# An expert layer's first product on 512-row tiles by seven quarter products instead of eight

## The chip, the cores and the metric

The kernel runs on one core of a Trainium2 chip. A core has five engines with a queue each: TensorE (PE in the profile; its weight loads are shown as PEld), VectorE (DVE), ScalarE (ACT), GpSimd (POOL) and SyncE (SP, which here only starts DMA transfers). Each works its queue in order, and they wait for each other by semaphores. Matmul results go to PSUM, of which this kernel uses eight banks of 128 x 512 float32, seven of them in one rotating pool.

The metric is the time of one execution in microseconds on the device. Three runs of the kernel before gave 1623.6 us as the median (1623.3 to 1626.15).

## The reference

Two blocks follow each other. The first is a filter along the sequence by a real Fourier transform (8 sequences of 2496 rows, 256 columns); the second a mixture of 8 experts with one expert for each row. All data is float32.

```python
X = np.fft.rfft(x, axis=1)
F = (filt_r + 1j * filt_i)[None, :, :]
y = np.fft.irfft(X * F, n=x.shape[1], axis=1)

x = y.reshape(B * S, D)                          # 19968 rows, D = 256
logits = x @ w_gate                              # 8 experts
expert_idx = np.argmax(logits, axis=1)
gate_w = softmax(logits)[arange(N), expert_idx]  # with 1e-9 in the denominator
for e in range(E):                               # the rows of expert e
    h = np.maximum(x_e @ w1[e], 0.0)             # 256 -> 1024
    y_e = h @ w2[e]                              # 1024 -> 256
out = gate_w[:, None] * y                        # in the rows' old order
```

## The kernel before

**Transform.** It is done as matmuls in four stages, A to D (`stage_a` to `stage_d`), for one of the eight sequences after the other; between the stages, data goes to DRAM and back in another layout (tensors `zd` and `ud`). Stage B multiplies its products by the filter with four VectorE operations (L366 to L370), and stage C reads the result. For the first sequence GpSimd does the fourth of them, and the layouts are changed by transposes in SBUF.

**Routing.** `turn_y`, `logits` and `route` take stage D's rows, choose the expert by many small VectorE operations and write each row, with its index and gate, into a DRAM table sorted by expert (`rows`), by indirect DMAs that GpSimd starts (L607, 128 rows or fewer each).

**Experts.** When the rows of one more sequence are in the table, `tile_map` finds which tiles of rows of one expert can be worked. A tile has 512, 256 or 128 rows. `GROUPS` sets their numbers ahead: 28 tiles of 512 rows, 14 of 256 and 23 of 128, the last two kinds mostly at the end. For each tile:

- `rows_in` loads the rows (`xg`), `weights` loads w1 and w2 of the expert in two halves each (`w1t`, `w2t`, 512 KB a half), all on SP's queue;
- `turn_x` transposes the rows (L737) into `xT`, which has the 256 columns of x as two blocks of 128 partitions, `dh`;
- `hidden(i, k)` makes 128 of the 1024 hidden columns for the whole tile: two matmuls, one for each `dh`, added up in a bank (L744), then a relu into `hT` on VectorE or ScalarE (L747, L748);
- `result(i, j)` makes 128 rows of output by eight matmuls with `hT` as weights and `w2t` as the moving side (L758), scales them with the gate (L762, L763) and writes them to their places with an indirect DMA of GpSimd (L764).

`turn_x` of the next tile stands between the last `hidden` and the first `result` of a tile where the rows have been loaded by then.

**Order of the work.** The order on TensorE, VectorE, ScalarE and SP is the order in which the program emits it. A loop at the end emits a step of the transform or one of the experts, by a simple clock of its own (`now`), costs written beside each step, and a credit: each transform step gives the experts `share()` times its cost. `either` picks VectorE or ScalarE for an evacuation by which would be free first in that clock. `side` emits pieces of routing between. `prefetch` emits the loads when a buffer count allows. GpSimd's order is left to the framework. When the transform is over, its memory is given to w1 buffers for the 128-row tiles (`late["w1"]`) and to all of w2.

Of the kernel before, what the change touches and what calls it, by code (L numbers as in the profile page):

```python
# [22 lines left out]
E = 8  # L23
# [111 lines left out]
def kernel(  # L135
# [215 lines left out]
    def stage_b(b, f):  # L351
# [11 lines left out]
        yw = sb.tile([P, 2, D], F32, tag="yw", name="yw")  # L363
# [261 lines left out]
    def tile_map(b, rows, n, last):  # L625
# [21 lines left out]
        tau = pools["moe"].tile([1, n], F32, tag=f"tau{n}", name="tau", bufs=1)  # L647
        past = pools["moe"].tile([1, n, E - 1], F32, tag=f"past{n}", name="past", bufs=1)
# [5 lines left out]
        ef = pools["moe"].tile([1, n], F32, tag=f"ef{n}", name="ef", bufs=1)  # L654
# [5 lines left out]
        rf = pools["moe"].tile([1, n], F32, tag=f"rf{n}", name="rf", bufs=1)  # L660
# [24 lines left out]
    work, idt, gts, xgs, xts, w1t, w2t, hs = [], {}, {}, {}, {}, {}, {}, {}  # L685
# [21 lines left out]

    def weights(h, second):
# [10 lines left out]
        if second:  # L719
            w2t[h] = pools["moe"].tile([P, FH2, D], F32, tag="w2t", name="w2t", bufs=3)  # L720
            nc.sync.dma_start(out=w2t[h], in_=moe_w2[bass.ds(ev, 1), k].rearrange("o p i d -> p (o i) d"))
        else:
            pool, bufs = (late["w1"], 8) if i >= SHORT else (pools["moe"], 3)
            w1t[h] = pool.tile([P, DH, F // 2], F32, tag="w1t", name="w1t", bufs=bufs)
            nc.sync.dma_start(out=w1t[h], in_=moe_w1[bass.ds(ev, 1), k].rearrange("o p i f -> p (o i) f"))

    def turn_x(i):
# [6 lines left out]
        for dh in range(DH):  # L734
# [3 lines left out]
            evac(xts[i][:, dh, :n * P].rearrange("p (j q) -> p j q", j=n), pt[:, :n], n * P)  # L738

    def hidden(i, k):  # L740
        m = work[i][0] * P
        p = bank()
        for dh in range(DH):
            mm(p[:, :m], lhsT=w1t[2 * i + k // FH2][:, dh, k % FH2 * P:(k % FH2 + 1) * P], rhs=xts[i][:, dh, :m],  # L744
               start=(dh == 0), stop=(dh == DH - 1))
        hT = pools["moe"].tile([P, 512], F32, tag="hT", name="hT", bufs=9)
        either(m, lambda: nc.vector.tensor_scalar_max(hT[:, :m], p[:, :m], 0.0),  # L747
               lambda: nc.scalar.activation(hT[:, :m], p[:, :m], AF.Relu))  # L748
        hs.setdefault(i, []).append(hT)

    def result(i, j):
# [4 lines left out]
        for k in range(FT):  # L756
            w2 = late["w2s"][:, bass.ds(ev, 1), k, :] if i >= SHORT else w2t[2 * i + k // FH2][:, k % FH2, :]
            mm(p[:, :D], lhsT=hs[i][k][:, j * P:(j + 1) * P], rhs=w2, start=(k == 0), stop=(k == FT - 1))  # L758
        ys = pools["moe"].tile([P, D], F32, tag="ys", name="ys", bufs=4)
# [126 lines left out]
    def experts():  # L886

        for i in range(NT):
# [18 lines left out]
    def share():  # L907

        known = sum(7.1 * t[0] for t in work[used["w2"] // 2:])
# [71 lines left out]
```

## Time and profile before

| | |
|---|---|
| median of three runs | 1623.6 us |
| profiled execution | 1628.1 us, of which its span is 1626.4 us |
| TensorE busy | 1570.7 us, 97% of the span |
| VectorE, ScalarE, GpSimd busy | 423.1, 518.5, 358.2 us |
| mean granted TensorE clock | 0.987 |
| first product of the experts, records of 512, 256 and 128 columns (L744) | 896, 448, 736 |
| second product of the experts (L758) | 2240 + 368 records |
| read from and written to HBM | 208.44 MB, 80.90 MB |

The profile is of one execution. A float32 matmul appears in it as two weight loads (LDWEIGHTS) and two MATMUL records. A line of a group gives the line of the kernel, engine, operation, what is written and read, the shape, the count, then busy us in all and mean ns of one, then the engine's idle time just before, with what ended it. Matmuls overlap in the pipeline, so a record's length is more than its share of the time; the pace is read from the starts. A line of the timeline gives start and length in us; "x32" is 32 instructions merged. A line of a table of stretches gives the bounds, the length, the busy time of PE, PEld, DVE, ACT and POOL with the number of instructions, then the granted TensorE clock, the DMA engines' busy share and GB/s.

### The profile page before, as it was taken

The page shows a single profiled execution, that of the slowest core. Times are in us where ns is not written, and L with a number is a line of the kernel's source. Part 1 is how long each engine was busy: PE and PEld are TensorE (multiplying, and loading weights), DVE is VectorE, ACT ScalarE, POOL GpSimd, SP SyncE. Part 2 cuts the span into 40 slices and gives each one's busy share as a digit, 9 for nine tenths or more (in the row PEclk, how much of TensorE's full clock was granted, in tenths as well). Part 3 has the DMA queues.
Part 4 walks back from the last instruction along what each step waited for, and adds up shares of the span by engine and source line. Part 5 has one row for each costly group of instructions (what it writes and reads, how often), then busy time and mean ns, then how long its engine had stood idle before and what let it go on. Part 6 is the DMA issues. An engine that isn't in the chain of part 4 may idle for free.

```text
span 1626.4 us, 21714 instructions
## 1 busy us (share of the span) xinstructions
PE 1570.7 (97%) x7094; PEld 1143.6 (70%) x7094; DVE 423.1 (26%) x1418; ACT 518.5 (32%) x1149; POOL 358.2 (22%) x373
## 2 busy tenths in 40 slices
PE   8988899999999999999999899999999999999998
PEld 6645667787566666666666566667666678889997
DVE  4676571624412422235222111300000000000000
ACT  4434343333322232322233232122222222333433
POOL 1131312404213321023213205411111011111111
PEclk9999999999999999999999999999999999999999
DMA  9679796887935584357434624433344347565551
GB/s 283 185 198 293 234 329 196 244 262 241 289 121 163 167 250 138 114 152 191 144 106 129 178 89 142 145 112 112 133 151 153 129 142 229 187 214 184 172 182 46
DMA packets 119700, 289.89 MB, mean 178 GB/s; under 512 B 17387, under 2 KB 58484, under 8 KB 119469
## 3 DMA queue, kind: packets, MB, share of 16 engines
q1 hardware_dynamic: 100373, 245.18, 49.9%
q0 software_dynamic: 19216, 43.33, 7.7%
q8 instruction: 58, 0.95, 0.2%
q14 instruction: 53, 0.43, 0.1%
HBM read 208.44 MB, written 80.90 MB: 178 GB/s over the span
## 4 chain that ended last, share of the span: by engine, by line
PE 90%; DMA 4%; DVE 3%; issue 2%; SPq 0%; ACT 0%; POOL 0%; POOLq 0%; ACTq 0%; DVEq 0%
PE bank L758 34%; PE bank L744 34%; PE bank L405 4%; PE bank L359 3%; PE bank L344 3%; PE bank L384 3%; PE bank L737 2%; PE bank L477 2%; DMA fin<-zd 1%; PE lt L491 1%; DMA fin<-ud 1%; DMA ud<-uo 1%; PE bank L424 1%; DVE yw L368 1%; DVE yw L367 1%
## 5 line engine op out<-in xcount | busy, mean ns | idle before, releaser
L744 PE MATMUL bank<-xT,w1t 128*128 128x512 f32 (+2 forms) x2080 | 592.0, 436 | 0.0
L758 PE MATMUL bank<-w2t,hT 128*128 128x256 f32 x2240 | 503.9, 382 | 2.6 <-issue 2.6
L744 PEld LDWEIGHTS bank<-xT,w1t 128*128 128x128 f32 x2080 | 338.9, 191 | 206.2 <-issue 183.7
L758 PEld LDWEIGHTS bank<-w2t,hT 128*128 128x128 f32 x2240 | 423.9, 191 | 70.2 <-issue 14.2
L764 POOL DMA_INDIRECT out_dram<-ys,idt x163 | 160.6, 985 | 917.2 <-ACT ys L763 624.4
L748 ACT ACTIVATE hT<-bank 128x512 f32<-128x512 f32 (+2 forms) x520 | 227.3, 438 | 369.3 <-PE bank L744 333.4
L607 POOL DMA_INDIRECT rows<-yo,row x176 | 175.5, 997 | 303.5 <-DVE row L587 73.6
L763 ACT ACTIVATE ys<-bank,gts 128x256 f32<-128x256 f32 x157 | 74.3, 474 | 500.0 <-PE bank L758 447.9
L241 DVE COPY xT<-bank 128x128 f32<-128x128 f32 (+2 forms) x53 | 25.1, 473 | 586.1 <-PE bank L737 459.6
L366 DVE TENSOR_TENSOR ys<-bank,ht 128x512 f32<-128x512 f32 x80 | 55.1, 689 | 131.0 <-PE bank L359 88.2
L405 PE MATMUL bank<-fin,tds 120*117 120x256 f32 (+1 forms) x308 | 77.6, 391 | 12.0 <-DMA fin<-ud 12.0
L758 PE MATMUL bank<-w2s,hT 128*128 x368 | 83.2, 379 | 0.0
L405 PEld LDWEIGHTS bank<-fin,tds 120*117 120x117 f32 (+1 forms) x308 | 55.6, 185 | 37.0 <-issue 20.4
L384 PE MATMUL bank<-ys,tcs 128*128 128x512 f32 x126 | 67.0, 614 | 10.8 <-DVE ys L370 6.1
L344 PE MATMUL bank<-fin,tas 117*120 117x512 f32 x154 | 74.5, 603 | 0.0
L758 PEld LDWEIGHTS bank<-w2s,hT 128*128 128x128 f32 x368 | 68.1, 190 | 8.3
L359 PE MATMUL bank<-fin,tbs 128*128 128x256 f32 x280 | 73.2, 385 | 0.8 <-DMA fin<-zd 0.8
L359 PEld LDWEIGHTS bank<-fin,tbs 128*128 128x128 f32 x280 | 52.3, 192 | 21.5 <-issue 15.5
L241 ACT COPY uo<-bank 128x512 f32<-128x512 f32 x70 | 41.1, 587 | 62.7 <-PE bank L384 36.7
L367 DVE SCALAR_TENSOR_TENSOR yw<-bank,ht 64x512 f32<-64x512 f32 x80 | 55.4, 693 | 1.1
L368 DVE TENSOR_TENSOR yw<-bank,ht 64x512 f32<-64x512 f32 x80 | 54.7, 684 | 1.1
L241 ACT COPY yo<-bank 117x512 f32<-117x512 f32 x70 | 40.6, 589 | 40.7 <-PE bank L405 38.5
(126 smaller groups left out, 877.6 us busy)
## 6 DMA issues: line engine op xcount, KB each, us to landing
w1t<-in_moe_w_dram SPq DMA_DIRECT2D x130, 512.0 KB
w2t<-in_moe_w_dram SPq DMA_DIRECT2D x84, 512.0 KB
fin<-in_x_dram SPq DMA_DIRECT2D x40, 512.0 KB
fin<-zd SPq DMA_DIRECT2D x70, 256.0 KB
ud<-uo SPq DMA_DIRECT2D x70, 256.0 KB
zd<-zo SPq DMA_DIRECT2D x35, 480.0 KB
fin<-ud SPq DMA_DIRECT2D x35, 480.0 KB
xg<-rows SPq DMA_DIRECT2D x28, 544.0 KB
```

The costliest lines, as they stand in the source:

```text
L241: either(n, lambda: nc.vector.tensor_copy(o, i), lambda: nc.scalar.copy(out=o, in_=i))
L344: mm(p[:TK, :], lhsT=tas, rhs=xt[:TP, j:j + 2, :], start=True, stop=True)
L359: mm(p[:, i * D:(i + 1) * D], lhsT=tbs[:, f + i, :], rhs=zi[:, j + i, :], start=True, stop=True)
L367: nc.vector.scalar_tensor_tensor(out=yw[:HP], in0=z2[HP:], scalar=-1.0, in1=fi, op0=ALU.mult, op1=ALU.mult)
L384: mm(p, lhsT=tcs[:, 1, :], rhs=ys, start=True, stop=True)
L405: mm(p[:TP, i * D:(i + 1) * D], lhsT=tds[:k, i0 + j + i, :], rhs=ui[:k, j + i, :], start=True, stop=True)
L607: sc = nc.gpsimd.indirect_dma_start(out=rowsd, out_offset=bass.IndirectOffsetOnAxis(ap=at, axis=0), in_=what, in_offset=None,)
L744: mm(p[:, :m], lhsT=w1t[2 * i + k // FH2][:, dh, k % FH2 * P:(k % FH2 + 1) * P], rhs=xts[i][:, dh, :m], start=(dh == 0), stop=(dh == DH - 1))
L748: lambda: nc.scalar.activation(hT[:, :m], p[:, :m], AF.Relu))
L758: mm(p[:, :D], lhsT=hs[i][k][:, j * P:(j + 1) * P], rhs=w2, start=(k == 0), stop=(k == FT - 1))
L763: lambda: nc.scalar.activation(ys, p[:, :D], AF.Copy, scale=gate))
L764: nc.gpsimd.indirect_dma_start(out=out, out_offset=bass.IndirectOffsetOnAxis(ap=idt[i].bitcast(U32)[:, j, :], axis=0), in_=ys, in_offset=None,
```

## The change

On tiles of 512 rows, `hidden` gives way to `hidden_by_quarters`. It works the hidden columns in two halves (`g`; with the new layout of w1 in DRAM, a half holds columns of both halves of F, `fh`). In each half, w1 is a matrix of 2 x 2 quarters (`dh` by `fh`, 128 x 256 each), and so is the transposed tile (`dh` by half of the rows, 128 x 256 each). Their product is made of seven quarter products in place of eight, in Winograd's form of Strassen's scheme. One quarter product is two matmuls of 256 columns into one bank.

The scheme needs four sums of quarters of x for each tile (at the end of `turn_x`) and four sums of quarters of w1 for each half (`w1_sums`), all on GpSimd. The seven products are put together by seven additions on VectorE, with a bank as one operand and SBUF as the other; the first product is copied to `part` by ScalarE, and the relu becomes two operations of ScalarE on 1024 elements a partition, in place in `hT`. `w1_sums` of the next half is emitted in the middle of a half where its weights have come by the program's clock, otherwise just ahead of its own half.

For the memory, `w2t` goes from 3 to 2 buffers, `xg` from 2 to 1 (4 in the late pool for the 128-row tiles), `ys` of `result` from 4 to 3, `yw` to one buffer after the first sequence, and the small tiles of `tile_map` are shared between sizes. `hT` becomes one tile for each half, in two buffers, and `result` takes its pieces in the same order of hidden columns as before. `share` reckons 26.8 for a 512-row tile in place of 28.4.

```diff
--- before.py
+++ after.py
@@ -360,7 +360,7 @@
         z2 = p.rearrange("p (i d) -> p i d", i=2)
         ys = outs["y", b, f] = sb.tile([P, 2, D], F32, tag="ys", name="ys", bufs=3)
-        yw = sb.tile([P, 2, D], F32, tag="yw", name="yw")
+        yw = (pro if b == 0 else sb).tile([P, 2, D], F32, tag="yw", name="yw", bufs=2 if b == 0 else 1)
...
+        most = max(m for group in GROUPS for _, m in group)
+        tau = pools["moe"].tile([1, most], F32, tag="tau", name="tau", bufs=1)[:, :n]
...
-        xg = xgs[i] = pools["moe"].tile([P, 4, DR], F32, tag="xg", name="xg")
+        xg = xgs[i] = (late["w1"] if i >= SHORT else pools["moe"]).tile([P, 4, DR], F32, tag="xg", name="xg", bufs=4 if i >= SHORT else 1)
...
         if second:
-            w2t[h] = pools["moe"].tile([P, FH2, D], F32, tag="w2t", name="w2t", bufs=3)
+            w2t[h] = pools["moe"].tile([P, FH2, D], F32, tag="w2t", name="w2t", bufs=2)
...
             pool, bufs = (late["w1"], 8) if i >= SHORT else (pools["moe"], 3)
-            w1t[h] = pool.tile([P, DH, F // 2], F32, tag="w1t", name="w1t", bufs=bufs)
-            nc.sync.dma_start(out=w1t[h], in_=moe_w1[bass.ds(ev, 1), k].rearrange("o p i f -> p (o i) f"))
+            w1t[h] = pool.tile([P, DH, 2, 2 * P], F32, tag="w1t", name="w1t", bufs=bufs)
+            nc.sync.dma_start(out=w1t[h], in_=moe_w1[bass.ds(ev, 1), k].rearrange("o p i h f -> p (o i) h f"))
...
             evac(xts[i][:, dh, :n * P].rearrange("p (j q) -> p j q", j=n), pt[:, :n], n * P)
-
-    def hidden(i, k):
+        if n == 4:
+
+            b = xts[i].rearrange("p h (r c) -> p h r c", r=2)
+            t = sums[i] = pools["moe"].tile([P, 4, 2 * P], F32, tag="sums", name="sums", bufs=1)
+            nc.gpsimd.tensor_tensor(t[:, 0], b[:, 0, 1], b[:, 0, 0], op=ALU.subtract)
+            nc.gpsimd.tensor_tensor(t[:, 1], b[:, 1, 1], t[:, 0], op=ALU.subtract)
+            nc.gpsimd.tensor_tensor(t[:, 2], b[:, 1, 1], b[:, 0, 1], op=ALU.subtract)
+            nc.gpsimd.tensor_tensor(t[:, 3], b[:, 1, 0], t[:, 1], op=ALU.subtract)
+            free["p"] = max(free["p"], now[0]) + 3.0
+
+    def w1_sums(h):
+
+        w = w1t[h]
+        t = wsum[h] = pools["moe"].tile([P, 4, 2 * P], F32, tag="wsum", name="wsum", bufs=2)
+        nc.gpsimd.tensor_tensor(t[:, 0], w[:, 0, 1], w[:, 1, 1], op=ALU.add)
+        nc.gpsimd.tensor_tensor(t[:, 1], t[:, 0], w[:, 0, 0], op=ALU.subtract)
+        nc.gpsimd.tensor_tensor(t[:, 2], w[:, 0, 0], w[:, 0, 1], op=ALU.subtract)
+        nc.gpsimd.tensor_tensor(t[:, 3], w[:, 1, 0], t[:, 1], op=ALU.subtract)
+        free["p"] = max(free["p"], now[0]) + 3.0
+
+    def hidden_by_quarters(h):
...
+        i = h // 2
+        w, ws, t = w1t[h], wsum[h], sums[i]
+        b = xts[i].rearrange("p h (r c) -> p h r c", r=2)
+        hT = pools["moe"].tile([P, 2, 2, 2, 2 * P], F32, tag="hT", name="hT", bufs=2)
+        hs.setdefault(i, []).append(hT)
+        part = pools["moe"].tile([P, 2, 2 * P], F32, tag="part", name="part", bufs=1)
+
+        def product(left, right):
+            q = bank().rearrange("p (v c) -> p v c", v=2)
+            for v in range(2):
+                mm(q[:, v], lhsT=left[:, v * P:(v + 1) * P], rhs=right, start=True, stop=True)
+            return q
+
+        def add(o, q, a):
+            nc.vector.tensor_tensor(o, q, a, op=ALU.add)
+            free["v"] = max(free["v"], now[0]) + 0.7
+
+        def relu(o, q):
+            nc.scalar.activation(o, q, AF.Relu)
+            free["s"] = max(free["s"], now[0]) + 0.6
+
+        low = hT[:, 1, :, 0]
+        q = product(w[:, 0, 0], b[:, 0, 0])
+        nc.scalar.copy(out=part, in_=q)
+        free["s"] = max(free["s"], now[0]) + 0.6
+        q = product(w[:, 1, 0], b[:, 1, 0])
+        add(hT[:, 0, :, 0], q, part)
+        yield 1.71
+        q = product(ws[:, 1], t[:, 1])
+        add(part, q, part)
+        q = product(ws[:, 2], t[:, 2])
+        add(low, q, part)
+        yield 1.71
+        q = product(ws[:, 0], t[:, 0])
+        add(hT[:, 1, :, 1], q, low)
+        add(part, q, part)
+        q = product(w[:, 1, 1], t[:, 3])
+        add(low, q, low)
+        relu(hT[:, 1], hT[:, 1])
+        yield 1.71
+        q = product(ws[:, 3], b[:, 1, 1])
+        add(hT[:, 0, :, 1], q, part)
+        relu(hT[:, 0], hT[:, 0])
+        yield 0.85
+
+    def hidden(i, g, a):
+
         m = work[i][0] * P
         p = bank()
+        fh, v = divmod(a, 2)
         for dh in range(DH):
-            mm(p[:, :m], lhsT=w1t[2 * i + k // FH2][:, dh, k % FH2 * P:(k % FH2 + 1) * P], rhs=xts[i][:, dh, :m],
+            mm(p[:, :m], lhsT=w1t[2 * i + g][:, dh, fh, v * P:(v + 1) * P], rhs=xts[i][:, dh, :m],
                start=(dh == 0), stop=(dh == DH - 1))
-        hT = pools["moe"].tile([P, 512], F32, tag="hT", name="hT", bufs=9)
-        either(m, lambda: nc.vector.tensor_scalar_max(hT[:, :m], p[:, :m], 0.0),
-               lambda: nc.scalar.activation(hT[:, :m], p[:, :m], AF.Relu))
-        hs.setdefault(i, []).append(hT)
+        if a == 0:
+            hs.setdefault(i, []).append(pools["moe"].tile([P, 2, 2, 2, 2 * P], F32, tag="hT", name="hT", bufs=2))
+        hT = hs[i][g][:, fh, v].rearrange("p r c -> p (r c)")[:, :m]
+        either(m, lambda: nc.vector.tensor_scalar_max(hT, p[:, :m], 0.0),
+               lambda: nc.scalar.activation(hT, p[:, :m], AF.Relu))
...
         for k in range(FT):
             w2 = late["w2s"][:, bass.ds(ev, 1), k, :] if i >= SHORT else w2t[2 * i + k // FH2][:, k % FH2, :]
-            mm(p[:, :D], lhsT=hs[i][k][:, j * P:(j + 1) * P], rhs=w2, start=(k == 0), stop=(k == FT - 1))
-        ys = pools["moe"].tile([P, D], F32, tag="ys", name="ys", bufs=4)
+            mm(p[:, :D], lhsT=hs[i][k % 4 // 2][:, k // 4, k % 2, j // 2, j % 2 * P:(j % 2 + 1) * P], rhs=w2, start=(k == 0), stop=(k == FT - 1))
+        ys = pools["moe"].tile([P, D], F32, tag="ys", name="ys", bufs=3)
...
         i = got["x"]
-        if i < len(work) and rows_at[work[i][3]] <= now[0] and i - used["x"] < 2:
+        if i < len(work) and rows_at[work[i][3]] <= now[0] and i - used["x"] < (1 if i < SHORT else 3):
...
             if h < 2 * len(work) and rows_at[work[h // 2][3]] <= now[0] and (
-                    h - used[what] < (3 if h < 2 * SHORT else 8)):
+                    h - used[what] < ((3 if what == "w1" else 2) if h < 2 * SHORT else 8)):
                 weights(h, what == "w2")
...
-            for k in range(FT):
-                yield lambda: hidden(i, k), 0.43 * n, ("w1", 2 * i + k // FH2)
-                if (k + 1) % FH2 == 0:
-                    w1t.pop(used["w1"])
-                    used["w1"] += 1
-            xts.pop(i)
+            for g in range(2):
+                h = 2 * i + g
+                if n == 4:
+                    if h not in wsum:
+                        yield lambda: w1_sums(h), 0.0, ("w1", h)
+                    steps = hidden_by_quarters(h)
+                    for m in range(4):
+                        yield lambda: next(steps), (1.71, 1.71, 1.71, 0.85)[m], ("w1", h)
+                        if m == 1 and when.get(("w1", h + 1), now[0] + 1.0) <= now[0] and TILES[(h + 1) // 2][0] == 4:
+                            w1_sums(h + 1)
+                    wsum.pop(h)
+                else:
+                    for a in range(4):
+                        yield lambda: hidden(i, g, a), 0.43 * n, ("w1", h)
+                w1t.pop(h)
+                used["w1"] += 1
+            xts.pop(i), sums.pop(i, None)
...
     def share():
-        known = sum(7.1 * t[0] for t in work[used["w2"] // 2:])
+        known = sum(26.8 if t[0] == 4 else 7.1 * t[0] for t in work[used["w2"] // 2:])
         return min(4.0, max(0.3, (known - RESERVE) / max(left_t[0], 1.0)))
...
-        moe_w1=inputs["moe_w1"].reshape(E, DH, P, 2, F // 2).transpose(0, 3, 2, 1, 4),
+        moe_w1=inputs["moe_w1"].reshape(E, DH, P, 2, 2, F // 4).transpose(0, 4, 2, 1, 3, 5),
```

More of the change, by code (lines that the diff above doesn't have):

```diff
@@ L646, in tile_map @@
         yield
-        tau = pools["moe"].tile([1, n], F32, tag=f"tau{n}", name="tau", bufs=1)
-        past = pools["moe"].tile([1, n, E - 1], F32, tag=f"past{n}", name="past", bufs=1)
+        most = max(m for group in GROUPS for _, m in group)
+        tau = pools["moe"].tile([1, most], F32, tag="tau", name="tau", bufs=1)[:, :n]
+        past = pools["moe"].tile([1, most, E - 1], F32, tag="past", name="past", bufs=1)[:, :n]
         she = (1, n, E - 1)
@@ L653, in tile_map @@
         yield
-        ef = pools["moe"].tile([1, n], F32, tag=f"ef{n}", name="ef", bufs=1)
+        ef = pools["moe"].tile([1, most], F32, tag="ef", name="ef", bufs=1)[:, :n]
         erow = pools["moe"].tile([1, n], I32, tag=f"erow{n}", name="erow", bufs=2)
@@ L659, in tile_map @@
         yield
-        rf = pools["moe"].tile([1, n], F32, tag=f"rf{n}", name="rf", bufs=1)
+        rf = pools["moe"].tile([1, most], F32, tag="rf", name="rf", bufs=1)[:, :n]
         rrow = pools["moe"].tile([1, n], I32, tag=f"rrow{n}", name="rrow", bufs=2)
@@ L682, in tile_map @@
         work.extend((rows // P, erow[0:1, i:i + 1], rrow[0:1, i:i + 1], b) for i in range(n))
-    work, idt, gts, xgs, xts, w1t, w2t, hs = [], {}, {}, {}, {}, {}, {}, {}
+    work, idt, gts, xgs, xts, w1t, w2t, hs, sums, wsum = [], {}, {}, {}, {}, {}, {}, {}, {}, {}
     FH2 = FT // 2
```

## The prediction

> **What bounds the kernel now.** I read the page first: the busy shares, then the slices.
>
> ```profile
> PE 1570.7 (97%) x7094; PEld 1143.6 (70%) x7094; DVE 423.1 (26%) x1418; ACT 518.5 (32%) x1149; POOL 358.2 (22%) x373
> PE   8988899999999999999999899999999999999998
> DVE  4676571624412422235222111300000000000000
> ```
>
> TensorE is busy 97% of the span, and VectorE does almost nothing after about two thirds of it: the transform is over and only expert tiles are left. The chain that ended last says the same.
>
> ```profile
> PE 90%; DMA 4%; DVE 3%; issue 2%; SPq 0%; ACT 0%; POOL 0%; POOLq 0%; ACTq 0%; DVEq 0%
> ```
>
> So matmul time taken away is worth its full length, unless a wait replaces it. Next, the groups with shapes kept apart, for the prices.
>
> ```profile
> L758 PE MATMUL bank<-w2t,hT 128*128 128x256 f32 x2240 | 503.9, 382 | 2.6 <-issue 2.6
> L744 PE MATMUL bank<-xT,w1t 128*128 128x512 f32 x896 | 401.3, 596 | 0.0
> L748 ACT ACTIVATE hT<-bank 128x512 f32<-128x512 f32 x224 | 133.8, 597 | 281.3 <-PE bank L744 253.2 <-issue 23.6 <-PE bank L359 4.5
> L366 DVE TENSOR_TENSOR ys<-bank,ht 128x512 f32<-128x512 f32 x80 | 55.1, 689 | 131.0 <-PE bank L359 88.2 <-issue 13.3 <-PE bank L744 9.4
> L370 POOL TENSOR_TENSOR ys<-ys,yw 128x512 f32<-128x512 f32 x10 | 12.7, 1268 | 40.0 <-DVE yw L368 26.8 <-PE bank L344 7.9 <-PE bank L359 5.2
> L435 ACT COPY ht<-ht 64x1024 f32<-64x1024 f32 x5 | 5.2, 1045 | 0.1
> ```
>
> A matmul is two records here (896 records for 28 tiles of 8 x 2 products). Their mean overlaps the next one, so the true pace comes from the timeline of TensorE in a stretch with expert tiles alone:
>
> ```profile
> 1084.49 13.90 PE L744 MATMUL bank<-xT,w1t 128*128 128x512 f32 x32
> 1098.23 1.04 PE L737 MATMUL bank<-ident,xg 128*128 128x128 f32 x8
> 1099.10 13.98 PE L758 MATMUL bank<-w2t,hT 128*128 128x256 f32 x64
> 1112.92 13.90 PE L744 MATMUL bank<-xT,w1t 128*128 128x512 f32 x32
> ```
>
> From start to start: first product 13.74 us (0.429 a record), transposes 0.87, second product 13.82 (0.216 a record of 256 columns); one tile 28.43 us, without a gap.
>
> [...]
>
> ```profile
> 752.16:755.57 3.41, 1.64 (x11) 1.42 (x10) 3.33 (x6) 0.10 (x1) 0.84 (x1) 1.00 0.44 135
> 755.57:758.98 3.41, 3.41 (x10) 2.70 (x9) 3.20 (x16) 0.49 (x1) 0.00 (x0) 0.50 1.13 250
> ```
>
> 1.77 us without matmuls in one window (1.64 busy of 3.41), and the next runs at clock 0.50. The same after 1.87 us at 410.82, but not after 1.54 us at 107.04. So a stall over some 1.7 us inside one window costs another 1.7 us. [...]
>
> ```profile
> 31.12 1.04 ACT L435 COPY ht<-ht 64x1024 f32<-64x1024 f32 x1
> 32.19 0.58 ACT L241 COPY zi<-bank 128x512 f32<-128x512 f32 x1
> ```
>
> 1.07 us from one start to the next.
>
> **The change, part by part.** Matmuls: 32 records of 512 columns (13.74) become 56 of 256 (7 products x 2 x 2, twice) at 0.216, 12.10 us. Weight loads of 191 ns still fit under 0.216, as in the second product. Saved: 1.64 us a tile, 28 tiles, 46 us.
>
> Evacuation: eight relus on ScalarE (8 x 0.597) become, per half of F, one copy (0.59) and two relus of 1024 elements from SBUF (1.07 each), and seven adds of 0.69 on VectorE. VectorE gets 9.7 us a tile, less than the 12.1 us of matmuls beside it, so it is no bound on average. But the order is strict. I follow one unmixed tile from the start of its first half. Products end every 0.864 us, the seventh at 6.05. A VectorE op starts 0.26 us after its matmul (transposes end at 1099.10, the copy starts 1099.36) and adds follow at 0.70 (0.72 when dependent). Product 5 ends at 4.32 and has two adds (4.58, 5.28), product 6 one (5.98), product 7 one (6.68 to 7.37). ScalarE: relu of the low part 6.71, of the high part 7.78 to 8.85. Only then the copy of the second half's first product, which was ready at 7.2: 8.85 to 9.43. That copy opens the second half's adds, which now run without a pause: 9.47, 10.17, 10.89, 11.61, 12.31, 13.01, 13.71 to 14.40. Relu low 13.74 to 14.78, relu high 14.81 to 15.86. TensorE ends its products at 12.10, does the transposes (12.97) and two matmuls of the second product (13.83); the third reads the tile that the last relu writes. It starts at 15.9: a stall of 2.1 us a tile. Bounds: 1.0 if the second half carried no backlog (the first half's relu ends 2.8 after its products; 1.73 is covered)[...]. Behind that matmul stands all of TensorE's queue. The seven banks are no limit: the last add is 2.3 us behind, under three products.
>
> Clock: a 2.1 us stall puts 1.7 us into one window at (3.41 - 2.1 + 2 x 0.4) / 3.41 = 0.62 of its positions, x 1.7 us = 1.05 us a tile; none below 1.7.
>
> Unmixed tiles. In the order as built, 12 of the 28 have no transform work among them: 12 x (-1.64 + 2.1 + 1.05) = +18 us.
>
> Mixed tiles. In the other 16, transform matmuls stand between the halves, or between last product and result, and shorten the wait; a stage B in a half puts 2.8 us of VectorE work in front of the adds and lengthens it. Walking each in the built order as above I get waits of 0 to 3 us, mean 0.8, so 13 us, plus 2 for the clock, against 26 saved: -11 us.
>
> GpSimd: [...] Weight sums are needed at the third product of a half and are issued a half earlier; those of x have the 13.8 us of the second product. Hidden when unmixed: behind the last scatter they end about 5 us into the tile, needed at 7.8. In front of them in POOL's queue can stand six to eight routing scatters (1.29 us each from start to start, 8 to 10 us), in about five tiles: 0 to 15 us, I take 3.
>
> VectorE's backlog also delays stage C, which waits for stage B's products there, and relus hold ScalarE's queue while they wait for adds: bounds 0 to 15, I take 5. It is 28% busy between 440 and 1010 us and would be about 50%.
>
> At nothing: the weights' DMA has the same size and pieces of the same length. Two w2 buffers in place of three: both halves load during the next first product (12 us for some 6 us of transfer; before, the second already waited for the result's end); uncovered, a few us a tile. One xg buffer: loaded a whole tile (26 us) ahead. ys 4 to 3, hT in two tiles, yw, map tiles: their readers finish before the next writer comes. The new constant in the share shifts which step comes next; bounded by the 23 us that TensorE waits for DMA now, either way a few us, taken as 0.
>
> Sum: 18 - 11 + 3 + 5 = +15 us. The profiled execution's span of 1626.4 us becomes 1641; it took 1628.1 as a whole, 4.5 above the median of 1623.6, to which I add the same: 1638 us.
>
> **Rivals.** (1) Faster: the relu arrives less late. One mechanism, at the third matmul of each first result: if the second half carries no backlog, unmixed stalls are 1.0 us and the clock stays up. 12 x (-0.64) - 11 - 2 + 5 = -16, about 1608; with more cover in mixed tiles 1600. It decides from a mean stall under 46/28 = 1.64 us. For it: ScalarE is 32% and VectorE 26% busy. Against: the copy stands behind two relus in the built order. (2) The stall comes, the clock doesn't fall: 15 - 14 = +1, about 1625. For it: a 2.35 us stall at 130 left the clock up; it lay across two windows. (3) VectorE or GpSimd becomes the bound while the transform runs: both upper ends, +22 more, about 1660. For it: stages with VectorE at 0.5 to 0.7 already. That quarter products don't run faster is ruled out by the 0.216.
>
> **Chances.** 0.2% (3 us) is about what a measurement of this kernel tells from no change. Main case 0.48 (1630 to 1652), rival 1 0.27, rival 2 0.15 (half of it within 0.2%, the rest to either side), rival 3 0.10. Faster 0.32, same 0.09, slower 0.59. The range, 1603 to 1662, leaves out the far ends of rivals 1 and 3.
>
> **What would show it.** Right: a gap of about 2 us before the first L832 matmuls in the unmixed tiles, released by ScalarE's relu, period 28.6 us or, with a fallen clock, 30.3; first product 12.1 us; VectorE's adds without a pause in the second half. Wrong: no gap there; or gaps before the third product, released by POOL; or before stage C, by VectorE.

## The result, and the profile after

The changed kernel takes 1675.6 us (median of 4 runs, 1674.3 to 1680.4) for 1624.9 us of the kernel before beside it (1623.3 to 1627.1): 1.032 times as long, 95% interval 1.029 to 1.034. The forecast of 1638 us had the sign right and the size wrong: +51 us, not +15, and outside the range. The profiled execution spans 1672.5 us; before, 1626.4. All that follows accounts for these 46.1 us.

The page of the changed kernel, its busy shares and four of its slices:

```profile
PE 1549.9 (93%) x7766; PEld 1278.4 (76%) x7766; DVE 691.8 (41%) x1789; ACT 535.6 (32%) x1114; POOL 597.9 (36%) x709
PE   8988979999899989998999998888999999999998
DVE  5585662634734474456655443344333330000000
POOL 2131433306434443345436546643444421111111
PEclk9998989999999999999999999998999999999999
```

TensorE works 20.8 us less and is idle 66.9 us more (122.6 us of the span, before 55.7). The granted clock was 0.976, before 0.987: at 1 minus the clock, times the span, that is 40.1 us, before 21.1. So three terms make the sum: 66.9 us of idle time, 19.0 us of lowered clock, and 39.8 us of matmul time saved, which is what remains (busy time less the clock's part: 1509.8 for 1549.6). 66.9 + 19.0 - 39.8 = 46.1.

The groups of instructions that are new, with what ended the idle time before them:

```profile
L832 PE MATMUL bank<-w2t,hT 128*128 128x256 f32 x2240 | 518.6, 388 | 45.2 <-ACT hT L784 42.3
L780 DVE TENSOR_TENSOR hT<-bank,part 128x512 f32<-128x512 f32 x168 | 115.4, 687 | 322.3 <-ACT part L789 161.2
L784 ACT ACTIVATE hT<-hT 128x1024 f32<-128x1024 f32 x112 | 113.8, 1051 | 297.7 <-DVE hT L780 273.1
L776 PE MATMUL bank<-sums,wsum 128*128 128x256 f32 x672 | 161.3, 386 | 9.5 <-POOL wsum L755 8.1
```

The second product (L832), which waited for no other engine before, waits 42.3 us for the relu that closes a half. The relu waits for the adds, the adds for the copy: a loop over three engines that the kernel before did not have. A wait of 8.1 us for GpSimd's sums stands apart from it.

Where it lies. I cut both traces at the same tiles, counted from 0, where their transposes start (the second product of the tile before comes just after them): tile 1, the first of 512 rows; tiles 2 to 22, five of 256 rows and sixteen of 512 among the transform's work; tiles 23 to 26; tiles 27 to 33, the last of 512 rows. Columns: the stretch, its length, then busy time of TensorE, its weight loads, VectorE, ScalarE and GpSimd, the clock and the DMA. First before, then after:

```profile
239.21:256.07 16.86, 16.86 (x42) 8.15 (x42) 4.78 (x24) 5.35 (x9) 7.90 (x8) 0.87 0.85 285
256.07:1007.79 751.72, 739.73 (x3138) 511.29 (x3136) 232.97 (x773) 233.03 (x472) 188.56 (x190) 0.99 0.58 173
1007.79:1126.65 118.86, 116.30 (x421) 77.82 (x420) 17.69 (x104) 28.74 (x53) 31.90 (x33) 0.99 0.39 127
1126.65:1325.61 198.96, 198.96 (x730) 133.48 (x729) 5.88 (x21) 50.02 (x91) 27.36 (x28) 1.00 0.41 139
```

```profile
237.42:264.04 26.62, 18.56 (x66) 14.89 (x66) 13.59 (x36) 4.52 (x7) 16.30 (x20) 0.74 0.69 212
264.04:1027.65 763.61, 724.14 (x3521) 585.70 (x3520) 382.72 (x975) 243.87 (x458) 326.18 (x382) 0.98 0.57 168
1027.65:1171.15 143.50, 120.37 (x517) 100.73 (x516) 58.38 (x162) 31.46 (x48) 69.28 (x85) 0.92 0.34 106
1171.15:1369.69 198.54, 189.30 (x897) 164.81 (x896) 73.00 (x120) 52.06 (x77) 84.07 (x108) 1.00 0.41 138
```

Tile 1 costs 9.8 us more, tiles 2 to 22 cost 11.9, tiles 23 to 26 cost 24.6, tiles 27 to 33 gain 0.4; before tile 1 it is -1.8, after tile 33 +2.0. (Which piece of the transform falls between which tiles differs a little, so the second and third figures are good to a few us.) Half of the loss is in four tiles in which TensorE has almost no transform work left. Most of the idle time there is the wait for the relu, once in each second product, 16.4 us of 23.1:

```profile
1033.39 14.70 PE L832 MATMUL bank<-w2t,hT 128*128 128x256 f32 x60 [3.69 <-ACT hT L784]
1067.94 16.18 PE L832 MATMUL bank<-w2t,hT 128*128 128x256 f32 x60 [5.58 <-ACT hT L784]
1103.39 14.90 PE L832 MATMUL bank<-w2t,hT 128*128 128x256 f32 x60 [3.69 <-ACT hT L784]
1143.06 16.17 PE L832 MATMUL bank<-w2t,hT 128*128 128x256 f32 x60 [3.41 <-ACT hT L784]
```

In tiles 2 to 22 this wait is 14.9 us. The other waits that are new there are for VectorE: 18.4 us in all (stage C 7.8, routing 5.0, transposes behind an add 4.2 and smaller ones) for 2.8 before, while those for DMA fell from 9.2 to 1.5.

At tile 1 TensorE waits for the sums of w1. GpSimd's queue, then TensorE's:

```profile
243.57 1.01 POOL L607 DMA_INDIRECT rows<-yo,row  x1 [3.88 <-DVE cnt L588]
244.61 0.73 POOL L754 TENSOR_TENSOR wsum<-w1t 128x256 f32<-128x256 f32 x1
...
247.33 0.71 POOL L755 TENSOR_TENSOR wsum<-wsum,w1t 128x256 f32<-128x256 f32 x1
```

```profile
248.10 4.45 PE L776 MATMUL bank<-sums,wsum 128*128 128x256 f32 x12 [6.13 <-POOL wsum L755]
```

The sums stood behind one routing scatter that itself waited 3.88 us for VectorE; those of the second half then stood behind five more scatters, and TensorE waited another 1.93 us.

One clean tile, on TensorE's timeline:

```profile
1171.15 1.04 PE L738 MATMUL bank<-ident,xg 128*128 128x128 f32 x8
1172.03 1.03 PE L832 MATMUL bank<-w2t,hT 128*128 128x256 f32 x4
1174.38 13.22 PE L832 MATMUL bank<-w2t,hT 128*128 128x256 f32 x60 [1.32 <-ACT hT L784]
1187.43 1.89 PE L776 MATMUL bank<-xT,w1t 128*128 128x256 f32 x8
```

The first product ran from 1159.07 to 1171.15, 12.08 us for 13.74 before: the seven products save what they should. The second product takes 15.40 us from start to start for 13.82: a gap of 1.32 us before its third matmul, and 0.26 us more. 1.66 saved, 1.58 given back. Every one of these seven tiles shows the same 1.32.

The four tiles (23 to 26) show why a loop over in-order queues is worse than its clean walk. GpSimd's timeline (the first and the last of routing's 14 scatters, then the first scatter of a result), then ScalarE's:

```profile
1063.81 1.01 POOL L607 DMA_INDIRECT rows<-yo,row  x1 [0.19 <-issue]
...
1083.06 0.97 POOL L607 DMA_INDIRECT rows<-fill,pad  x1 [0.31 <-issue]
1084.34 0.99 POOL L838 DMA_INDIRECT out_dram<-ys,idt  x1 [0.30 <-issue]
```

```profile
1080.77 0.47 ACT L837 ACTIVATE ys<-bank,gts 128x256 f32<-128x256 f32 x1 [2.99 <-PE bank L832]
1089.22 0.47 ACT L837 ACTIVATE ys<-bank,gts 128x256 f32<-128x256 f32 x1 [7.98 <-DMA out_dram<-ys,idt]
1089.60 0.58 ACT L789 COPY part<-bank 128x512 f32<-128x512 f32 x1
```

The results of a tile were ready from 1073.5 us on, but their scatters stood behind 20 us of routing's scatters. The fourth result found none of the three `ys` buffers free, ScalarE's queue stood 7.98 us, and behind it stood the copy that opens the next tile's adds. One tile later it is VectorE:

```profile
1120.13 0.69 DVE L780 TENSOR_TENSOR hT<-bank,part 128x512 f32<-128x512 f32 x1 [10.34 <-ACT part L789]
...
1124.29 0.14 DVE L630 TENSOR_TENSOR av<-cnt,done 1x8 f32<-1x8 f32 x1
1124.46 0.70 DVE L631 TENSOR_SCALAR av_i<-av 1x8 int32<-1x8 f32 x1
1125.20 0.65 DVE L632 TENSOR_SCALAR av_i<-av_i 1x8 int32<-1x8 int32 x1
...
1127.85 0.67 DVE L780 TENSOR_TENSOR hT<-bank,hT 128x512 f32<-128x512 f32 x1
```

Between the third and the fourth add of a half, 1124.29 to 1127.85, stands routing's list of tiles, ten small instructions; others stand before the second and after the sixth. The seven adds of that half took from 1120.13 to 1132.91, not 5. Four of the ten were slow: L631, L632, L636 and L641 took 0.65 to 0.70 us beside GpSimd's sums of 1124.42 to 1127.3, and 0.14 to 0.19 in the list before, from 1108.25 on. The adds, with one input from PSUM, took 0.68 to 0.69 us in the clean tiles, beside the sums and without them.

### The profile page after: what moved, and what is told of

The parts are those of the page before. It is cut to its first block, busy times and chain, and to the rows that moved or that the text cites. A ratio compares the mean times of both kernels' runs of the same rounds, so it can differ in the third digit from the quotient of the medians.

```text
span 1672.5 us, 23856 instructions
## 1 busy us (share of the span) xinstructions
PE 1549.9 (93%) x7766; PEld 1278.4 (76%) x7766; DVE 691.8 (41%) x1789; ACT 535.6 (32%) x1114; POOL 597.9 (36%) x709
## 5 line engine op out<-in xcount | busy, mean ns | idle before, releaser
L832 PE MATMUL bank<-w2t,hT 128*128 128x256 f32 x2240 | 518.6, 388 | 45.2 <-ACT hT L784 42.3
L832 PEld LDWEIGHTS bank<-w2t,hT 128*128 128x128 f32 x2240 | 427.7, 194 | 125.4 <-ACT hT L784 53.2
L780 DVE TENSOR_TENSOR hT<-bank,part 128x512 f32<-128x512 f32 x168 | 115.4, 687 | 322.3 <-ACT part L789 161.2
L784 ACT ACTIVATE hT<-hT 128x1024 f32<-128x1024 f32 x112 | 113.8, 1051 | 297.7 <-DVE hT L780 273.1
L817 PE MATMUL bank<-xT,w1t 128*128 128x128 f32 (+1 forms) x1184 | 189.6, 315 | 0.0
L817 PEld LDWEIGHTS bank<-xT,w1t 128*128 128x128 f32 x1184 | 169.9, 191 | 17.2 <-issue 4.9
L776 PE MATMUL bank<-sums,wsum 128*128 128x256 f32 x672 | 161.3, 386 | 9.5 <-POOL wsum L755 8.1
L776 PEld LDWEIGHTS bank<-sums,wsum 128*128 128x128 f32 x672 | 128.7, 193 | 32.5 <-POOL wsum L755 8.9
L241 DVE COPY xT<-bank 128x128 f32<-128x128 f32 (+2 forms) x44 | 18.4, 419 | 248.6 <-PE bank L738 171.4
L823 ACT ACTIVATE hT<-bank 128x128 f32<-128x128 f32 (+1 forms) x296 | 94.1, 318 | 82.3 <-PE bank L817 70.9
L776 PE MATMUL bank<-xT,w1t 128*128 128x256 f32 x448 | 108.7, 386 | 0.0
L776 PEld LDWEIGHTS bank<-xT,w1t 128*128 128x128 f32 x448 | 85.9, 194 | 16.2 <-issue 2.7
L832 PE MATMUL bank<-w2s,hT 128*128 x368 | 83.2, 379 | 0.0
L780 DVE TENSOR_TENSOR part<-bank,part 128x512 f32<-128x512 f32 x112 | 76.6, 684 | 13.7 <-PE bank L776 9.7
L780 DVE TENSOR_TENSOR hT<-bank,hT 128x512 f32<-128x512 f32 x112 | 76.7, 685 | 8.6 <-PE bank L776 5.2
```

Of the source, the lines that this page charges most:

```text
L776: mm(q[:, v], lhsT=left[:, v * P:(v + 1) * P], rhs=right, start=True, stop=True)
L780: nc.vector.tensor_tensor(o, q, a, op=ALU.add)
L784: nc.scalar.activation(o, q, AF.Relu)
L817: mm(p[:, :m], lhsT=w1t[2 * i + g][:, dh, fh, v * P:(v + 1) * P], rhs=xts[i][:, dh, :m], start=(dh == 0), stop=(dh == DH - 1))
L823: lambda: nc.scalar.activation(hT, p[:, :m], AF.Relu))
L832: mm(p[:, :D], lhsT=hs[i][k % 4 // 2][:, k // 4, k % 2, j // 2, j % 2 * P:(j % 2 + 1) * P], rhs=w2, start=(k == 0), stop=(k == FT - 1))
```

## The experiments

The runs came from several chips, on which the kernel before takes 1612 to 1625 us; ratios are each to the kernel before on the same chip, and expectations in microseconds were meant for the first one, so I divide them by 1623.6. Times of single tiles are from the profiled executions, one for each run, so differences of a few us between them are not sharp. Four theories were held against each other. A: the relu at a tile's end is late for the result that reads it. B: ScalarE is held by a `ys` that waits for a scatter. C: GpSimd's sums cost the time. D: routing's work stands in a heap between VectorE's adds.

**Order of the reads.**

```diff
-        for k in range(FT):
+        for k in (0, 1, 4, 5, 6, 7, 2, 3):
...
-... start=(k == 0), stop=(k == FT - 1))
+... start=(k == 0), stop=(k == 3))
```

> The changed kernel with one edit: a result reads the eight chunks of hT in the order 0, 1, 4, 5, 6, 7, 2, 3, so that the quarters whose relu comes last are read seventh and eighth and not third and fourth. Theory A, the late relu at the end of a tile is the main loss: the third matmul of a tile's first result waited 42.3 us in all, and each such wait is 1.32 us in a clean tile; the two relus of the last half would have 1.7 and 2.6 us of matmuls ahead of them instead of 0.87, so the clean tile falls from 28.36 to 26.9 us and the whole to 1635 to 1650. Theory B, ScalarE is held by a ys that waits for a scatter, and what is late is the whole chain of adds, by more than a tile's end can hide: the waits of 3 to 6 us between 1027 and 1171 us stay, only the clean tiles gain, 8 x 1.4 us, and the time is 1655 to 1665.

Measured: 1.0047 (1.0029 to 1.0065), where the changed kernel has 1.0316: some 44 us less, a larger gain than theory A's range (1.007 to 1.016) allowed. TensorE's waits for the relu (total, times, longest), and a clean tile:

```profile
PE bank L832 <- ACT hT L784: 10.6, 7, 4.2
```

```profile
1157.65 1.04 PE L738 MATMUL bank<-ident,xg 128*128 128x128 f32 x8
1158.52 13.98 PE L832 MATMUL bank<-w2t,hT 128*128 128x256 f32 x64
1172.34 1.89 PE L776 MATMUL bank<-xT,w1t 128*128 128x256 f32 x8
```

The wait for the relu fell from 42.3 us in 24 places to 10.6 in 7, the gap in the clean tile is gone and the 0.26 us with it (the second product takes 13.82 us from start to start), its period is 26.77 us. Theory A holds: which quarter is read third decides most of the time. The gain is larger than the 31.7 us of idle time. The rest is of the size of 17 times 0.26 us and of the clock (0.980 for 0.976, some 8 us). But tiles 23 to 26 took 133.2 us, and tile 1 took 26.4: something else holds these.

**The sum in place, and five buffers of `ys`.** `part` goes; the copy goes to the quarter of `hT` that is written fourth, the running sum to the one written last.

```diff
-        nc.scalar.copy(out=part, in_=q)
+        nc.scalar.copy(out=hT[:, 1, :, 1], in_=q)
...
+        part = hT[:, 0, :, 1]
...
-        ys = pools["moe"].tile([P, D], F32, tag="ys", name="ys", bufs=3)
+        ys = pools["moe"].tile([P, D], F32, tag="ys", name="ys", bufs=5)
```

> The changed kernel without the tile part: the first product is copied into the quarter of hT that is written fourth, and the running sum stands in the quarter that is written last. The room goes to ys, 5 buffers for 3. Theory B, ys is short of buffers: ScalarE's wait of 8 us for a scatter's landing at 1081 to 1089 us is gone, with it most of the 22.6 us of PE idle and 10 us of half clock in the four tiles from 1027 to 1171 us, and the time is 1645 to 1660. Theory A, the late relu at a tile's end: nothing of that changes but the wait of a copy for the last reader of part; 1670 to 1677.

> The changed kernel without the tile part, with ys left at 3 buffers: the half of the run with ys 5 (1.022 times the kernel before) that has no more room for ys. If the gain of that run on the changed kernel (1.032) came from the buffers of ys, this one is at 1.028 to 1.033; if it came from the copy's wait for the last reader of part, which ends 0.2 us sooner in each clean tile, it is at 1.021 to 1.025.

Measured: 1.0219 (1.0189 to 1.0249) with five buffers, 1.0264 (1.0238 to 1.0290) with three. The two together stand at the dear end of theory B's 1.013 to 1.022. Each half is worth some 0.5%. The run with three buffers lies between the two ranges given for it, and the intervals of the two runs touch, so the share of `ys` alone is not sharp. ScalarE's wait of 8 us is gone with five buffers, yet tiles 23 to 26 still took 137.1 us: theory B's wait was real and was not the main thing there; VectorE's heap, which this leaves alone, remained. The clean tile fell to 28.17 us, the gap to 1.12.

**No sums.** The twelve GpSimd instructions of a tile are dropped and plain quarters multiplied in the place of the sums, so the kernel leaves out what the sums compute.

```diff
-        nc.gpsimd.tensor_tensor(t[:, 0], w[:, 0, 1], w[:, 1, 1], op=ALU.add)
... (and the other seven lines)
+        wsum[h] = w.rearrange("p i h f -> p (i h) f")
```

> The changed kernel without the twelve sums of a tile on GpSimd: the products take plain quarters of w1 and x in their place (so what they compute is left out, and the output is another). Theory C, GpSimd's time is what was lost: the wait of 8.06 us for wsum at 238 to 257 us and its half clock go (12 us), and scatters of results come sooner, so that ScalarE isn't held; 1640 to 1655. Theories A and B say that the sums hide everywhere but at that one place: 1660 to 1667.

Measured: 1.0122 (1.0090 to 1.0153), in theory C's 1.010 to 1.019: tile 1 took 18.6 us, tiles 23 to 26 took 123.2. VectorE was busy 661.2 us for 691.8 with the same adds and routing.

**The buffers alone, then the sums beside eight products.** In the kernel before: `w2t` 2, `xg` 1, `ys` 3, `yw` as in the changed kernel; in the second run also twelve sums a tile into a tile that nobody reads.

```diff
-        ys = pools["moe"].tile([P, D], F32, tag="ys", name="ys", bufs=4)
+        ys = pools["moe"].tile([P, D], F32, tag="ys", name="ys", bufs=3)
...
+        t = pools["moe"].tile([P, 2 * P], F32, tag="idle", name="idle", bufs=1)
+        for u, v in ((a, b), (c, b), (c, a), (d, b)):
+            nc.gpsimd.tensor_tensor(t, u, v, op=ALU.subtract)
```

> The kernel before with the buffers of the changed one and nothing else: w2t 2 for 3, xg 1 for 2, ys 3 for 4, with the limits of the loads that go with them, and the yw of the later batches 1 for 2. If the buffers alone cost time, as theory B has it, some of the loss between 1000 and 1170 us appears here: 1632 to 1645. If the buffers cost nothing without the quarters (relu and ys are then dealt out to two engines, and one that is held doesn't hold the tile), 1622 to 1630.

> The kernel before with the changed one's buffers (1.0044 times the kernel before) and, beside its eight products, the twelve sums of a tile on GpSimd, written to a tile that nobody reads. Theory C in its wide form, the sums cost by holding scatters and VectorE's small instructions whatever the products are: 1.010 to 1.020. Rival, they cost only where the products wait for them and the relus form a chain: 1.003 to 1.007.

Measured: 1.0044 (1.0023 to 1.0065) and 1.0028 (1.0013 to 1.0043). Fewer buffers cost some 0.4%, just above the range given for "nothing" (0.999 to 1.004). The sums cost nothing on top, although they made GpSimd busy 604.8 us for 358.0 and VectorE 447.8 for 424.8 with the same instructions. So the wide form of theory C falls: the sums are free beside eight products, and dear only to a kernel whose products wait for them and whose adds stand in VectorE's queue.

**The order, joined with ys, with sums on VectorE, and without sums.**

```diff
-            nc.gpsimd.tensor_tensor(t[:, 0], b[:, 0, 1], b[:, 0, 0], op=ALU.subtract)
+            nc.vector.tensor_tensor(t[:, 0], b[:, 0, 1], b[:, 0, 0], op=ALU.subtract)
... (all eight)
```

> The new order of reads (1.005 times the kernel before) and no part with ys 5 (1.022) in one kernel. If they take away different waits, the late relu at a tile's end and the ys that waits for a scatter, their gains on 1.032 add up: 0.993 to 0.998. If the new order already covers what ys 5 covered, and the rest is VectorE and GpSimd, it stays at 1.000 to 1.006.

> The new order of reads with the twelve sums of a tile on VectorE in place of GpSimd. A sum of 128 x 256 is some 0.36 us there by half of the 0.69 us of a 128 x 512 one, so 4.3 us a tile for the 8.7 us on GpSimd. Theory C, the sums hold GpSimd's queue (scatters of results and of routing behind them) and lengthen the small VectorE instructions that run beside them[...]: tile 1's wait of 7.8 us goes, the four tiles after 998 us lose 10 us or more, and the ratio is 0.985 to 0.998. Rival, VectorE is the engine that is short and gets 4.3 us more in each tile ahead of its adds: 1.005 to 1.015.

> The new order of reads with the sums left out (plain quarters are multiplied in their place, so what they compute is left out). The bound for every place that the sums can be put: theory C expects that the gains of the two edits add up (1.032 to 1.005 and to 1.012), so 0.985 to 0.990. If the sums cost mostly by making relus late that the new order has covered already, 0.995 to 1.003.

Measured: 1.0047 (1.0032 to 1.0063) with `ys` 5, so nothing in the whole on top of the order. It is not shown that the order had covered it: tiles 23 to 26 fell from 133.2 us to 124.1, but tiles 2 to 22 took 750.9 for 739.5, on another chip. The other two runs keep three buffers. Without sums 0.9933 (0.9917 to 0.9950), a miss of both ranges that lies between them: the sums' gain of 1.9% in the changed kernel shrinks to 1.1% with the new order. With the sums on VectorE 1.033 (1.0305 to 1.0355), worse than its rival's range: all of the order's gain is lost. A sum takes 0.42 us there, 5.0 us a tile, and a clean tile shows

```profile
1224.17 1.89 PE L832 MATMUL bank<-w2t,hT 128*128 128x256 f32 x8
1228.04 14.04 PE L832 MATMUL bank<-w2t,hT 128*128 128x256 f32 x56 [1.97 <-ACT hT L784]
```

a gap of 1.97 us even in the new order, now before the fifth of the eight matmuls. The 56 records behind it take 13.87 us from start to start, for 12.10 at 0.216 each. The period is 30.70 us, 1.70 more than 26.77 with the gap and its 0.26 would make; by my estimate that is one stretch of 3.41 us at a clock of 0.50. The mean clock of this run is 0.970, with the new order alone 0.980. On VectorE's timeline the four sums of a half stand between its third and fourth add (1246.17 to 1247.64), and the adds behind them come later by them. VectorE is busy 45% of the span, and yet its order sets these tiles.

**Routing in small pieces, and the late relus.** Once the transform's steps are given out, one piece of routing after each step of the experts; and the first half's relus after the second half's copy.

```diff
-            for _ in range(4):
+            for _ in range(4 if f else 1):
                 side()
...
-        relu(hT[:, 0], hT[:, 0])
+        if h % 2:
+            relu(hT[:, 0], hT[:, 0])
+        else:
+            owed["relu"] = [lambda: relu(hT[:, 1], hT[:, 1]), lambda: relu(hT[:, 0], hT[:, 0])]
```

> New order of reads and ys 5 without part (1.005 times the kernel before), and once the transform's steps are all given out, one piece of routing's work after each step of the experts in place of four. Theory D, what is lost in the four tiles from 1017 to 1141 us is VectorE's routing work in a heap between two adds: these tiles take 124.1 us for some 108 and fall to 110 to 118, ratio 0.996 to 1.001. Rival, the loss is GpSimd's (the scatters of the last rows and the sums behind them): 123 to 126 us as before, 1.003 to 1.007.

> New order of reads and ys 5 without part (1.005 times the kernel before), and the two relus of a tile's first half given to ScalarE after the copy of the second half's first product. If the copy behind the two relus (2.0 us) is what still makes the adds late in mixed tiles: 0.995 to 1.001. If with the new order nothing waits for these adds: 1.003 to 1.007.

> The changed kernel with one edit: one piece of routing's work after each step of the experts in place of four, once the transform's steps are all given out. Theory D, VectorE's routing work in a heap between two adds made the loss of 24.6 us in the four tiles from 1027 to 1171 us: they take 143.5 us and fall to 115 to 122, ratio 1.015 to 1.021. Theory B, it was ScalarE held by a ys that waits for a scatter behind routing's scatters: they stay at 135 or more, 1.026 or more.

Measured: small pieces on top of order and `ys` 5, 0.9979 (0.9965 to 0.9993), tiles 23 to 26 at 110.1 us for 124.1, clock 1.00: theory D, as expected, though tiles 27 to 33 took 192.8 for 187.4. Late relus on top of order and `ys` 5, 0.9996 (0.9984 to 1.0009): as expected for "the copy behind the relus makes adds late in mixed tiles". Small pieces alone in the changed kernel, 1.0273 (1.0243 to 1.0302): tiles 23 to 26 fell to 118.7 us as theory D said, but the whole missed its range. Part of the work that was spread now stands later: the second products of tiles 26 to 28 wait 3.8, 3.8 and 4.9 us for the relu, and the stretch of tiles 27 to 33 took 214.9 us for 198.5. With the old order of reads the heap on VectorE was for the most part only moved on. The stretch before tile 1, which the edit leaves as it was, also took 8.6 us more in this execution. Tiles 23 to 26 lose most of their excess without the sums (123.2 us) and with small pieces (118.7) alike, so what the sums and the heap cost there overlaps and is not to be added up.

**Quarters in some tiles only.**

```diff
+    QUARTERS = {i for i in range(NT) if TILES[i][0] == 4 and i >= 27}
...
-                if n == 4:
+                if i in QUARTERS:
```

> New order of reads and ys 5 without part, with the seven products only in the seven 512-row tiles that come after all of the transform's and routing's work, and eight products of 256 columns' halves, as in the kernel before, in the 21 tiles ahead of them. Theory: the gain of 1.65 us a tile is whole where no other work shares VectorE and GpSimd, 7 x 1.65 = 11.6 us, less the 0.2 to 0.4 per cent that fewer buffers of w2t and xg cost: 0.993 to 0.998. If a tile that starts the quarters costs as tile 1 did: 1.000 or more.

> All that helped together: new order of reads, no part with ys 5, relus of a first half after the copy, one piece of routing a step at the end, and the seven products only from the eighth tile on, so that the first tiles, where the sums queue behind routing's scatters, have eight. If the start of the quarters at tile 1 cost what it showed (26.4 us for 18.5): 0.985 to 0.993. If the first tile with quarters waits as long wherever it stands: 0.994 to 0.999.

Measured: on top of the new order and `ys` 5, with quarters in the seven clean tiles alone, 0.9962 (0.9949 to 0.9974), those tiles 187.4 us for 199.0, 11.6 us as worked out, TensorE busy without a pause. With the new order, `ys` 5, late relus, small pieces, and quarters from the eighth tile on, 0.9866 (0.9837 to 0.9894), 1604.4 us for 1624.8, in the first of its two ranges: faster than both kernels. Even so only some 20 us of the 45 that 27 tiles of 1.65 us hold arrive.

Its profiled execution was the slowest of five (1614.7 us). In it tile 1, with eight products, took 21.0 us, 4.7 of them a wait for the rows of the next tile (`xg`). Tiles 2 to 22 have 19.7 us of idle time and 11.4 of lowered clock (the kernel before: 12.0 and 6.8). Tiles 27 to 33 took 198.4 us, as long as with eight products: in one of them GpSimd's sums stood behind a scatter that waited 5.9 us for an earlier one to land, and TensorE waited 6.2 us for the sums.

The largest waits over the whole run are for DMA (9.3 us for `xg`, 8.4 for `ud`), for VectorE at stage C (12.7), for GpSimd's sums in that one place (6.2) and for routing (5.9). Three kernels with eight products in the transform's time (the kernel before, the one with fewer buffers, and the one with quarters in the last seven tiles) show 4.5 to 9.3 for `xg`, 10.6 to 14.0 for `ud`, 5.9 to 10.9 for stage C and 1.6 to 4.0 for routing. So the waits for DMA are not owed to the quarters; how the rest of the missing 25 us divides stays open.

## Why the prediction was right or wrong

- **The saving.** 12.10 us for the first product was forecast, 12.08 measured. 46 us was forecast in all, 39.8 came. The sum left out the 0.26 us that came beside the gap of a wait; at the 24 waits for the relu that would be 6.2 us, which is reckoned from the clean tiles and not measured at each.
- **The stall at the tile's end.** Right in place, cause and releaser, too large in size: 1.32 us, not 2.1, in clean tiles. I had adds follow at 0.70 to 0.72 and relus at 1.07; on the timeline independent adds follow at 0.60, dependent ones at 0.8, and the second relu starts 0.96 after the first, so that the pair takes 2.00. The 1.07 us read from one copy out of SBUF did not hold for two relus. So the second product ran on 15.3 us after the tile's start and not 15.9. The mean of 0.8 us in mixed tiles was right: tiles 2 to 22 hold the second products of 16 tiles of 512 rows and 14.9 us of this wait, 0.9 each.
- **The clock.** 1.05 us a clean tile was my estimate from the traces of before; 1.32 us of gap cost none in seven of seven tiles, as rival 2 had it. In the traces before and after, the granted clock is 1.00 or 0.50, and its changes lie whole multiples of 3.413 us apart; the prediction's two lines are such stretches. Of the stretches at 1.00 behind the first matmuls, all with 1.77 us or more without matmuls (9 before, 17 after) were followed by one at 0.50, and none with 1.75 or less. The gap of 1.75 us after the last clean tile lay in one stretch, 1370.94 to 1374.35, and the clock stayed at 1.00. In the run with 1.97 us of gap the tile's period of 30.70 us is nine such stretches, 30.72; so by my estimate the gap meets the same place of the grid in each tile, and not some share of its places. The lowered clock that did come is in tile 1 (4.6 us more than before), tiles 2 to 22 (5.1) and tiles 23 to 26 (10.2), after longer waits.
- **The step that failed.** It is the price of other engines' work in front of the chain: the terms "In front of them in POOL's queue" ("0 to 15 us, I take 3") and "VectorE's backlog" with "relus hold ScalarE's queue" ("bounds 0 to 15, I take 5"), and "ys 4 to 3", which was put at nothing. 8 us were set down for all of it. That the sums would hide rested on my estimate of a sum's time on GpSimd; they took 0.73 us each, 8.8 us a tile. In place of the 8 us the runs showed: at tile 1 the wait for sums behind routing's scatters cost 8.1 us of idle time and 4.6 us more of clock. In tiles 2 to 22 the waits other than the relu's grew by 12.6 us (27.5 more idle, less 14.9), those for VectorE from 2.8 to 18.4. Tiles 23 to 26 lost 24.6 us; one routing piece at a time took 24.8 us off these four, and put 16.4 us on the seven behind them.
- **The wrong reading behind it.** I counted 12 tiles as unmixed because TensorE had no transform work among them. Routing's work on VectorE and GpSimd ran through four of them, and there the walk with empty queues didn't hold: the stall was 3.4 to 5.6 us and not 2.1. At -1.64 + 2.1 + 1.05 each, tiles 23 to 33 were to cost 17 us; seven of them gave -0.4 and four +24.6. That leaves some -2 us of the forecast for tiles 1 to 22, which cost 21.7. So most of the miss is in the tiles among the transform's work, where no run parts the waits further, and the right sign is in part luck.
- **The rivals.** Rival 1 has its mechanism half confirmed: the stall was less late and the clock stayed up, but at 1.58 us with its 0.26 it ate the whole 1.66. The mean stall was 42.3/28 = 1.51 us, under the 1.64 that was to decide for a faster kernel, and the kernel was slower: that line left out the 0.26 us and all other waits. Rival 3, VectorE as the bound, was the nearest in size (1660); its place was not the transform's phase alone. What ought to have warned me stood in the page of before: VectorE's 26th slice of 40, 1016 to 1057 us, still has a 3, where I already reckoned with expert tiles alone.

## What to carry to other kernels

When one PSUM eviction becomes a chain of evictions over two engines, ask at which consumer the chain's last link is read, and let it be read last: here a permutation of eight reads was worth 2.7% of the kernel, about as much as the whole saving in matmuls. Call a stretch undisturbed only if all queues of the chain are free in it, not TensorE's alone, for in an in-order queue any foreign wait (a buffer behind a scatter, a heap of small bookkeeping operations) becomes a wait of the chain. And price a wait by what it adds from start to start (here 1.58 us for a gap of 1.32) and by the granted clock behind it, not by its gap.

## What the runs showed of the hardware

Beside GpSimd's sums four small VectorE instructions of the changed kernel took 0.65 to 0.70 us, for 0.14 to 0.19 in the list before. With the sums VectorE was busy 23 us more with eight products (447.8 for 424.8) and 31 us more with seven (691.8 for 661.2), but the adds from PSUM took 0.68 to 0.69 us beside the sums and without them. A gap in the matmuls of 1.32 us left the granted clock at 1.00 in seven of seven tiles, as did one of 1.75 us after them; behind one of 1.97 us, 56 records took 13.87 us for 12.10. Half the elements took more than half the time: a 128 x 256 sum of two SBUF tiles took 0.42 us on VectorE with the sums there, where half of a 512-element one is 0.35 (L370 before, 0.693), and 0.73 us on GpSimd, where half of one is 0.63 (L370 before, 1.268).
